# Two VectorE products of Q moved in front of the sums of A's squares, in a kernel whose attention runs under a mixture of experts

## The chip, the core and the metric

The kernel runs on one core of one Trainium2 chip. The metric is the device time of one launch in microseconds. Three runs of the kernel before took 1014.55, 1015.66 and 1016.92 us; their median, 1015.66 us, is the time that the changed kernel is set against.

## The reference, cut to what matters

There are two stages. The first is a linear attention with a complex, per-position decay; the second puts every token through all four experts of a two-layer network and weights the results.

```
mag   = sqrt(a_re^2 + a_im^2);  scale = min(mag, 0.999) / (mag + 1e-6)
ar, ai = a_re * scale, a_im * scale
for t in range(768):                     # state S is complex, 48 x 48 per batch and head
    S_re, S_im = ar*S_re - ai*S_im + k[t] v[t]^T,  ar*S_im + ai*S_re
    y[t] = q[t] . S_re
x   = y as 3072 rows of 384
p   = probs / (sum(probs) + 1e-9)
out = sum over e of p[e] * (relu(x @ w1[e]) @ w2[e])
```

All data are float32; batch 4, heads 8, head size 48, hidden size 1024.

## The kernel before

The 3072 positions are cut into twelve groups of 256 (g = 0 to 11), each of two chunks of 128. In place of the recurrence the kernel works with prefix products of the decay: with A the running complex product of a inside a chunk, the state at a position is A times a sum of k v^T / A, so that attention becomes Q = A q, K = A k / |A|^2 and ordinary matrix products of Q and K.

For each group the work that prepares Q and K runs in this order, mostly on VectorE and ScalarE. `norm` scales a to the allowed magnitude (its ScalarE steps are L320, L321, L331, L332, L337, L339 and L343, its VectorE steps L322, L338, L341, L344, L346). `prefix` forms the running products on VectorE: seven steps (L354 to L357), five doubling steps and a last "fm" step of six products (L305 to L310, 128x651). `finish` then has two parts. `head` lets ScalarE square both parts of A (L416, L417), lets VectorE sum the squares chunk by chunk (L420, below called the reductions), lets ScalarE form 1/|A|^2 by a logarithm and an exponential (L422, L423), and lets VectorE multiply A by q, one product for the real and one for the imaginary part (L425, the Q products). `tail` lets VectorE refine the reciprocal and multiply it by k (L439 to L441) and form the two parts of K (L443).

Q and K then change their layout by way of HBM: SyncE issues Q to `q_d` (L453) and `q_d` back to `Qst` (L460), and likewise `k_d` and `Kst`. `attention` has TensorE transpose K (L494), form state increments (L512), scores from `Qst` and `Kst` (L524) and outputs (L538, L543). Its result y goes to HBM (L611) and comes back as `xa` (L159), and ScalarE and VectorE split it into two parts, `xha` and `xla` (L166, L168). Groups 2 to 5 (`HALF`) send Q and K chunk by chunk, groups 6 to 11 whole.

The expert layers run beside this. For each group TensorE makes eight steps over the hidden size of the first two experts: `w1_step` (L179, into `ph`), then ScalarE's relu (L188, `hh`), VectorE's remainder (L189, `hl`), and `w2_step` (L198, into `po`), which is queued one step later. The attention of group g runs inside the expert steps of group g - 1. A generator hands out the pieces of `norm`, `prefix`, `head` and `tail` at a rate set by constants (`STEP`, `MORE`, `FIRST` and the number that each `yield` carries). The other two experts run at the end for all groups (L836 to L860).

The order of instructions on each engine is not the order in the source alone. A planner takes the traced program, simulates it with its own costs, and issues, engine by engine, what is ready, earlier source first. `behind(ins, prev)` adds an edge of order alone: `ins` stands later than `prev` in its engine's queue and waits for nothing. Each engine works its queue in order, and SyncE issues its transfers in order too. The scratch tiles of `norm`, `prefix` and `finish`, and the tile Q, share four buffers of one tag; a new tile waits until an old one of them is free, and Q's is free when its trip to `q_d` has landed.

Of the kernel before, what the change touches and what calls it, by code (L numbers as in the profile page):

```python
# [11 lines left out]
ALU = mybir.AluOpType  # L12
# [9 lines left out]
C = 128  # L22
# [35 lines left out]
NSEL = 2  # L58
# [10 lines left out]
def fast_path(ctx, tc, qkP, aP, vP, probsP, w, out, flag):  # L69
    nc = tc.nc  # L70
# [38 lines left out]
    def behind(ins, prev):  # L109
        tc.add_manual_dep(ins.ins, prev.ins.name,  # L110
                          mybir.DependencyInfo(mybir.DependencyClass.NoSync, mybir.DependencyReason.DATA),
                          reason="issue order")
# [116 lines left out]
    with ExitStack() as c1:  # L229
# [4 lines left out]
        def tmp(name):  # L234
            return big.tile([P, 2, NJ * G], F32, tag="tmp", name=name, bufs=TMP)
# [30 lines left out]
        def load_a(g, parts=((0, SEG),), prev=None):  # L266
            A = big.tile([P, 2, SEG, MS], F32, tag="A", name=f"A{g}", bufs=NA)
            src = aP[g].rearrange("p (c i m) -> p c i m", c=2, i=SEG)
            for lo, hi in parts:
                for c in range(2):  # L270
                    ins = nc.sync.dma_start(A[:, c, lo:hi], src[:, c, lo:hi])
                    if prev is not None:
                        behind(ins, prev)
            return A

        def load_qk(g, prev=None):
            t = big.tile([P, 2, SEG, MS], F32, tag="qk", name=f"qk{g}", bufs=1)
            src = qkP[g].rearrange("p (c i m) -> p c i m", c=2, i=SEG)
            for c in range(2):
                ins = nc.sync.dma_start(t[:, c], src[:, c])  # L280
                if prev is not None:
                    behind(ins, prev)
            return t
# [106 lines left out]
        def finish(g, A, qk):  # L390
            s = tmp(f"s2{g}")
            u = tmp(f"u2{g}")
            Q = big.tile([P, 2, NR, C + 1], F32, tag="tmp", name=f"Q{g}", bufs=TMP)
            K = []

            def im(ap):
                return ap.rearrange("p (i m) -> p i m", i=SEG)

            def some(ap, lo, hi):
                if hi - lo == CG:  # L400
                    return ap.rearrange("p i m -> p (i m)")
                return ap.rearrange("p i (j c s) -> p i j c s", j=NJ, c=CG)[:, :, :, lo, :]

            def rows(ap, lo, hi):
                if hi - lo == CG:
                    return ap.rearrange("p i (n s) -> p i n s", s=CS)
                return some(ap, lo, hi)

            def dst(ap, lo, hi):
                x = ap.rearrange("p n (i s) -> p i n s", i=SEG)  # L410
                return x if hi - lo == CG else x[:, :, lo::CG, :]

            a2a, i0a, b2a, ta = im(s[:, 0]), im(u[:, 0]), im(s[:, 1]), im(u[:, 1])

            def head(lo, hi):
                nc.scalar.activation(some(a2a, lo, hi), some(A[:, 0], lo, hi), AF.Square)  # L416
                nc.scalar.activation(some(b2a, lo, hi), some(A[:, 1], lo, hi), AF.Square)  # L417
                for c in range(lo, hi):
                    a2, ic = some(a2a, c, c + 1), some(i0a, c, c + 1)
                    red = nc.vector.tensor_tensor_reduce(a2, a2, some(b2a, c, c + 1), scale=1.0, scalar=3e38,  # L420
                                                         op0=ALU.add, op1=ALU.min, accum_out=st_a2[:, c, g:g + 1])
                    nc.scalar.activation(ic, a2, AF.Ln, scale=2.0 ** A2_LOG[c], bias=a2b)  # L422
                    last_act = nc.scalar.activation(ic, ic, AF.Exp, scale=-1.0, bias=a2e[:, c:c + 1])  # L423
                for c in range(2):
                    ins = nc.vector.tensor_tensor(dst(Q[:, c, :, :C], lo, hi), rows(A[:, c], lo, hi),  # L425
                                                  rows(qk[:, 0], lo, hi), op=ALU.mult)
                    if g < NSEL and lo == 1:
                        behind(ins, red)
                if hi == CG:
                    nc.scalar.activation(Q[:, :, :, C].rearrange("p c (j n) -> p c j n", n=CG),  # L430
                                         A[:, :, SEG - 1, NS - 1::NS].unsqueeze(3).broadcast_to([P, 2, NJ, CG]),
                                         AF.Copy)
                return last_act

            def tail(lo, hi):
                if not K:
                    K.append(big.tile([P, 2, NR, C], F32, tag="K", name=f"K{g}", bufs=1))
                a2, i0, t, kn = (some(x, lo, hi) for x in (a2a, i0a, ta, qk[:, 1]))
                nc.vector.tensor_tensor(t, a2, i0, op=ALU.mult)  # L439
                nc.vector.scalar_tensor_tensor(t, t, 2.0, i0, op0=ALU.subtract, op1=ALU.mult)  # L440
                nc.vector.tensor_tensor(t, kn, t, op=ALU.mult)  # L441
                for c in range(2):
                    last_dve = nc.vector.tensor_tensor(dst(K[0][:, c], lo, hi), rows(A[:, c], lo, hi), rows(ta, lo, hi),  # L443
                                                       op=ALU.mult)
                return last_dve

            return Q, K, head, tail

        def trip(nm, X, dst, lo=0, hi=CG, prev=None):
# [210 lines left out]
        A = [load_a(0, halves)]  # L660
        wst = {i: stage1(i, PRE) for i in range(NST)}
        qk = load_qk(0)
# [150 lines left out]
    with ExitStack() as c2:  # L813
# [51 lines left out]
        for r in range(NT // T2):  # L865
            xh, xl = load_x2(r)
            prev = [fin.tile([P, C2, HD], F32, name=f"prev{e}") for e in range(E1)]
# [209 lines left out]
```

## Time and profile before

| What | Value |
|---|---|
| median of three runs | 1015.66 us (1014.55 to 1016.92) |
| the profiled execution's own time | 1011.7 us |
| its span | 1009.9 us |
| TensorE (PE) busy | 979.9 us, 97% |
| weight loads (PEld) | 921.2 us, 91% |
| VectorE (DVE) busy | 590.5 us, 58% |
| ScalarE (ACT) busy | 364.2 us, 36% |
| granted clock of TensorE, whole span | 0.994 |

The span is the time from the first to the last instruction of the program; the own time is what the run's clock gave for the same execution. Busy time says how long an engine had an instruction in it. The last 450 us of the span hold the two experts at the end, where VectorE and ScalarE have little to do, so that their shares over the whole span tell little of the stretch from 110 to 560 us, in which groups 2 to 11 are prepared.

### The profile page before, as it was taken

How to read it: one execution, taken by the hardware profiler on the slowest of the kernel's cores; microseconds unless marked ns; L12 is line 12 of the kernel's file. 1: busy time of each engine (PE TensorE's matmuls, PEld its weight loads, DVE VectorE, ACT ScalarE, POOL GpSimd, SP SyncE). 2: the span in 40 equal slices, each digit the busy share in tenths (PEclk: the TensorE clock that was granted, in tenths of full speed). 3: DMA queues.
4: the chain of work that ended last, by engine and by line, in shares of the span. 5: the costliest groups of instructions: out<-in, count | busy, mean ns of one | idle time of the engine just before them, and what ended most of it. 6: DMA issues, size and time to landing. Idle time of an engine off the chain costs nothing.

```text
span 1009.9 us, 16264 instructions
## 1 busy us (share of the span) xinstructions
PE 979.9 (97%) x6624; PEld 921.2 (91%) x6624; DVE 590.5 (58%) x1229; ACT 364.2 (36%) x653; POOL 34.2 (3%) x64
## 2 busy tenths in 40 slices
PE   4799999999999999999999999999999999999997
PEld 2699999999999999999999999999999899989996
DVE  7798988899988978798942463232132322321221
ACT  7756426446264462636422352121111211211110
POOL 5020000000000000000000000000000000000000
PEclk9899999999999999999999999999999999999999
DMA  9474366573774846547161780020030110100001
GB/s 317 151 148 147 80 160 159 152 187 108 166 184 131 211 96 172 153 123 211 55 168 39 249 307 32 1 94 32 1 126 1 39 56 1 63 1 1 32 1 35
DMA packets 88532, 110.76 MB, mean 110 GB/s; under 512 B 5824, under 2 KB 72944, under 8 KB 88448
## 3 DMA queue, kind: packets, MB, share of 16 engines
q1 hardware_dynamic: 84160, 94.50, 33.4%
q0 software_dynamic: 4288, 15.13, 5.0%
q8 instruction: 54, 0.88, 0.4%
q14 instruction: 30, 0.25, 0.1%
HBM read 73.70 MB, written 35.90 MB: 109 GB/s over the span
## 4 chain that ended last, share of the span: by engine, by line
PE 92%; DVE 2%; ACT 2%; DMA 2%; POOL 1%; issue 0%; DVEq 0%; POOLq 0%; SPq 0%
PE pob L849 20%; PE phb L836 20%; PE ph L179 20%; PE po L198 19%; PE sc L524 4%; PE dp L512 3%; PE yp L543 2%; PE yp L538 2%; PE ktp L494 1%; PE xp L574 1%; DMA mask_d<-mask 1%; DMA maskp<-mask_d 0%; PE qp L385 0%; POOL maskp L246 0%; DMA xa<-y_d 0%
## 5 line engine op out<-in xcount | busy, mean ns | idle before, releaser
L842 DVE SCALAR_TENSOR_TENSOR hlb<-phb,hhb 128x512 fp32r<-128x512 f32 x96 | 66.3, 691 | 270.6 <-ACT hhb L841 270.6
L841 ACT ACTIVATE hhb<-phb 128x512 fp32r<-128x512 f32 x96 | 57.4, 598 | 314.4 <-PE phb L836 299.1
L849 PE MATMUL pob<-wlo,hhb 128*128 128x384 f32 x384 | 129.2, 337 | 0.0
L198 PE MATMUL po<-whi,hh 128*128 128x384 f32 x384 | 129.2, 338 | 0.0
L849 PE MATMUL pob<-whi,hhb 128*128 128x384 f32 x384 | 128.9, 336 | 0.0
L198 PE MATMUL po<-wlo,hh 128*128 128x384 f32 x384 | 128.7, 335 | 0.0
L198 PE MATMUL po<-whi,hl 128*128 128x384 f32 x384 | 124.1, 338 | 0.7 <-DVE hl L189 0.6
L849 PE MATMUL pob<-whi,hlb 128*128 128x384 f32 x384 | 120.4, 336 | 0.0
L188 ACT ACTIVATE hh<-ph 128x512 fp32r<-128x512 f32 x96 | 57.2, 596 | 155.2 <-PE ph L179 145.9
L179 PE MATMUL ph<-xha,whi 128*128 128x256 f32 x576 | 104.5, 287 | 0.8 <-ACT xha L166 0.8
L179 PE MATMUL ph<-xha,wlo 128*128 128x256 f32 x576 | 101.5, 283 | 0.0
L179 PE MATMUL ph<-xla,whi 128*128 128x256 f32 x576 | 101.1, 284 | 0.0
L189 DVE SCALAR_TENSOR_TENSOR hl<-ph,hh 128x512 fp32r<-128x512 f32 x96 | 66.0, 687 | 55.8 <-ACT hh L188 55.4
L836 PE MATMUL phb<-xhb,whi 128*128 128x512 f32 x288 | 91.8, 392 | 0.0
L179 PEld LDWEIGHTS ph<-xha,whi 128*128 128x128 f32 x576 | 86.0, 190 | 2.0 <-ACT xha L166 1.0
L179 PEld LDWEIGHTS ph<-xha,wlo 128*128 128x128 f32 x576 | 83.0, 190 | 0.2 <-issue 0.2
L836 PE MATMUL phb<-xlb,whi 128*128 128x512 f32 x288 | 82.8, 392 | 0.0
L179 PEld LDWEIGHTS ph<-xla,whi 128*128 128x128 f32 x576 | 82.6, 191 | 0.0
L836 PE MATMUL phb<-xhb,wlo 128*128 128x512 f32 x288 | 82.3, 393 | 0.0
L849 PEld LDWEIGHTS pob<-whi,hhb 128*128 128x128 f32 x384 | 72.1, 188 | 3.6
L849 PEld LDWEIGHTS pob<-wlo,hhb 128*128 128x128 f32 x384 | 72.1, 188 | 3.3
L198 PEld LDWEIGHTS po<-whi,hh 128*128 128x128 f32 x384 | 72.4, 189 | 0.4 <-issue 0.3
(165 smaller groups left out, 1569.8 us busy)
## 6 DMA issues: line engine op xcount, KB each, us to landing
wst<-w SPq DMA_DIRECT2D x25, 384.0 KB, 6.1
qk<-qkP SPq DMA_DIRECT2D x24, 384.0 KB, 7.2
acc_d<-acc POOLq DMA_DIRECT2D x24, 384.0 KB, 4.4
prev<-acc_d SPq DMA_DIRECT2D x24, 384.0 KB, 4.7
A<-aP SPq DMA_DIRECT2D x22, 384.0 KB, 8.2
q_d<-Q SPq DMA_DIRECT2D x12, 387.0 KB, 4.1
Qst<-q_d SPq DMA_DIRECT2D x12, 387.0 KB, 6.1
v<-vP SPq DMA_DIRECT2D x24, 192.0 KB, 2.4
```

Of the source, the lines that this page charges most:

```text
L179: ins = nc.tensor.matmul(ph[:, u, :], wt[:, j * P:(j + 1) * P], xt[:, j, :], start=(n == 0), stop=(n == 3 * NJ - 1))
L188: wts["hh"] = nc.scalar.activation(hh, ph, AF.Relu)
L189: nc.vector.scalar_tensor_tensor(hl, ph, 0.0, hh, op0=ALU.max, op1=ALU.subtract)
L198: nc.tensor.matmul(po[t], ht[:, u, t * P:(t + 1) * P], wt[:, HD:], start=(i % FE == 0 and n == 0), stop=(i % FE == FE - 1 and n == 2))
L512: nc.tensor.matmul(d_ps[:, h, :], KT[:, h, :], vc[:, h * D:(h + 1) * D], start=True, stop=True)
L524: nc.tensor.matmul(s_ps[:, h, :], Kc[:, hf * 4 + h, :], Qc[:, hf * 4 + h, :], start=True, stop=True)
L538: ins = nc.tensor.matmul(yo, st[:, o:o + n], Qc[:, o // D, :], start=True, stop=False)
L543: ins = nc.tensor.matmul(yo, vc[:, o:o + n], sc[h // 4][:, h % 4, :], start=first, stop=True)
L836: nc.tensor.matmul(ph, wt[:, j * P:(j + 1) * P], xt[:, j, :], start=(n == 0), stop=(n == 3 * NJ - 1))
L841: nc.scalar.activation(hh, ph, AF.Relu)
L842: nc.vector.scalar_tensor_tensor(hl, ph, 0.0, hh, op0=ALU.max, op1=ALU.subtract)
L849: ins = nc.tensor.matmul(po[t], ht[:, t * P:(t + 1) * P], wt[:, HD:], start=(i % FE == 0 and n == 0), stop=(i % FE == FE - 1 and n == 2))
```

## The change

From group 2 on (`NSEL` is 2) the two Q products are traced directly behind the two squares and in front of the reductions, and an edge of order puts each reduction behind the second product. Groups 0 and 1 keep the old order. No instruction is added or taken away, no size and no buffer changes.

```diff
+                def products(prev=None):
+                    for c in range(2):
+                        ins = nc.vector.tensor_tensor(dst(Q[:, c, :, :C], lo, hi), rows(A[:, c], lo, hi),
+                                                      rows(qk[:, 0], lo, hi), op=ALU.mult)
+                        if prev is not None:
+                            behind(ins, prev)
+                    return ins
+
+                if g >= NSEL:
+                    q = products()
                 for c in range(lo, hi):
                     a2, ic = some(a2a, c, c + 1), some(i0a, c, c + 1)
                     red = nc.vector.tensor_tensor_reduce(a2, a2, some(b2a, c, c + 1), scale=1.0, scalar=3e38,
                                                          op0=ALU.add, op1=ALU.min, accum_out=st_a2[:, c, g:g + 1])
+                    if g >= NSEL:
+                        behind(red, q)
                     nc.scalar.activation(ic, a2, AF.Ln, scale=2.0 ** A2_LOG[c], bias=a2b)
                     last_act = nc.scalar.activation(ic, ic, AF.Exp, scale=-1.0, bias=a2e[:, c:c + 1])
-                for c in range(2):
-                    ins = nc.vector.tensor_tensor(dst(Q[:, c, :, :C], lo, hi), rows(A[:, c], lo, hi),
-                                                  rows(qk[:, 0], lo, hi), op=ALU.mult)
-                    if g < NSEL and lo == 1:
-                        behind(ins, red)
+                if g < NSEL:
+                    products(red if lo == 1 else None)
```

## Rows read from the trace of the kernel before

**Rows 1.** Busy time by stretch: length, engines (instructions), granted clock, DMA share, GB/s.
```profile
110.00:560.00 450.00, 446.98 (x3627) 434.76 (x3626) 362.61 (x792) 208.43 (x383) 10.27 (x19) 1.00 0.55 142
```
**Rows 2.** Waits of TensorE, 110 us to the end: total us, times, longest us.
```profile
PE sc L524 <- issue: 1.5, 2, 0.9
PE ph L179 <- ACT xha L166: 0.8, 1, 0.8
PE po L198 <- DVE hl L189: 0.6, 1, 0.6
```
**Rows 3.** VectorE by line and shape, 110:560: busy us, mean ns | idle before, releaser.
```profile
L425 DVE TENSOR_TENSOR Q<-A,qk 128x768 f32<-128x768 f32 x20 | 18.2, 952 | 0.0
L420 DVE CUSTOM_DVE_ANT_1 s<-s 128x384 f32<-128x384 f32 x20 | 10.4, 555 | 7.5 <-ACT s L417 7.4
L338 DVE TENSOR_TENSOR u<-s,u 128x768 f32<-128x768 f32 x9 | 8.6, 954 | 2.0 <-ACT u L337 1.9
```
**Rows 4.** Waits of ScalarE, 110:560.
```profile
ACT u L332 <- DMA q_d<-Q: 8.9, 6, 2.3
```
**Rows 5.** Timeline of VectorE, group 6: start us, us, instruction [idle before <-releaser].
```profile
279.44 0.83 DVE L310 TENSOR_TENSOR A<-fm_1a,fm_1b 128x651 f32<-128x651 f32 x1
282.79 0.56 DVE L420 CUSTOM_DVE_ANT_1 s<-s 128x384 f32<-128x384 f32 x1 [2.52 <-ACT s L417]
...
284.36 1.82 DVE L425 TENSOR_TENSOR Q<-A,qk 128x768 f32<-128x768 f32 x2
...
292.73 0.69 DVE L189 SCALAR_TENSOR_TENSOR hl<-ph,hh 128x512 fp32r<-128x512 f32 x1 [1.28 <-ACT hh L188]
...
294.34 1.82 DVE L443 TENSOR_TENSOR K<-A,u 128x768 f32<-128x768 f32 x2
```
**Rows 6.** Timeline of ScalarE, group 6.
```profile
288.42 0.92 ACT L331 ACTIVATE s<-s,m2b 128x768 f32<-128x768 f32 x1
...
291.27 0.94 ACT L332 ACTIVATE u<-s,lnb 128x768 f32<-128x768 f32 x1 [1.93 <-DMA q_d<-Q]
292.12 0.58 ACT L188 ACTIVATE hh<-ph 128x512 fp32r<-128x512 f32 x1
```
**Rows 7.** Timeline of SyncE, group 6: issues of transfers.
```profile
295.32 1.24 SPq L453 DMA_DIRECT2D k_d<-K  x2
298.35 1.31 SPq L460 DMA_DIRECT2D Kst<-k_d  x2
```
**Rows 8.** Timeline of TensorE, the first scores of group 6.
```profile
306.46 2.02 PE L524 MATMUL sc<-Qst,Kst 112*128 112x128 f32 x16 [0.86 <-issue]
```
**Rows 9.** Timeline of VectorE, group 2.
```profile
116.53 0.55 DVE L420 CUSTOM_DVE_ANT_1 s<-s 128x384 f32<-128x384 f32 x1
...
126.04 0.96 DVE L338 TENSOR_TENSOR u<-s,u 128x768 f32<-128x768 f32 x1 [0.73 <-ACT u L337]
```
**Rows 10.** Timeline of ScalarE, group 2.
```profile
124.19 0.94 ACT L332 ACTIVATE u<-s,lnb 128x768 f32<-128x768 f32 x1 [1.58 <-DMA q_d<-Q]
```
**Rows 11.** Timeline of TensorE, the first scores of group 2.
```profile
135.29 1.91 PE L524 MATMUL sc<-Qst,Kst 112*128 112x128 f32 x15 [0.64 <-issue]
```
**Rows 12.** Timeline of VectorE, group 4.
```profile
195.93 0.56 DVE L420 CUSTOM_DVE_ANT_1 s<-s 128x384 f32<-128x384 f32 x1 [0.67 <-ACT s L417]
```
**Rows 13.** Timeline of ScalarE, group 4.
```profile
198.54 0.85 ACT L166 ACTIVATE xha<-xa 128x768 fp32r<-128x768 f32 x1 [2.63 <-DMA xa<-y_d]
199.29 0.60 ACT L422 ACTIVATE u<-s,a2b 128x384 f32<-128x384 f32 x1
```
**Rows 14.** Timeline of SyncE, group 4.
```profile
213.82 1.07 SPq L460 DMA_DIRECT2D Kst<-k_d  x2
```
**Rows 15.** DMA issues of 213.5:215, group 4: KB each, median us to landing.
```profile
Kst<-k_d SPq DMA_DIRECT2D x2, 192.0 KB, 3.8
```
**Rows 16.** Timeline of TensorE, the first scores of group 4.
```profile
218.94 2.02 PE L524 MATMUL sc<-Qst,Kst 112*128 112x128 f32 x16
```
**Rows 17.** The nine loads of `xa` by source line L159, from issue to landing.
```profile
DMA to landing us min/median/max: 3.2/3.4/6.6
```

## The prediction

> **What bounds the kernel now.** I read the table of stretches first. Between 110 and 560 us, where groups 2 to 11 are prepared, TensorE has an instruction in it for 446.98 of 450 us, while VectorE is busy for 362.61, which is 81%, and ScalarE for 208.43 [rows 1]. The reader should see that TensorE sets the pace there, and that VectorE is busy but has 87 us to spare. After 560 us the change has no instruction.
>
> The waits of TensorE come second, because only they can be shortened by a new order on VectorE. From 110 us to the end there are four: two in front of scores, 1.5 us together, one of 0.8 us for `xha`, and one of 0.6 us for `hl` [rows 2], in all 2.9 us of a span of 1009.9. That is the ceiling of what the profile lets this change win.
>
> Third I looked at the waits that the change touches directly. VectorE stands idle for 7.4 us in front of the reductions, because they need ScalarE's squares; the twenty Q products, 952 ns each, stand behind them and wait for nothing [rows 3]. One step further on, ScalarE stands idle for 8.9 us, six times, in front of the exponential of the next `norm`, until a trip of Q to `q_d` has landed and Q's buffer is free [rows 4]. Everything behind that exponential on ScalarE, the relu of the experts among it, is held up as well.
>
> **The change part by part.** Nothing is added. Twenty products of 952 ns [rows 3] change places with twenty reductions, two against two in each of ten groups.
>
> *VectorE's own time.* A pair of Q products takes 1.82 us, two reductions about 1.1 us (2 x 555 ns). In group 6 VectorE ends the prefix at 280.27 and waits until 282.79 for the squares [rows 5]. The pair fits into these 2.52 us, the reductions start when they did before, and Q is ready at 282.09 instead of 286.18. Over the ten groups the idle time that can be filled is at most 7.4 us. On TensorE that is worth nothing by itself, since VectorE has 87 us to spare.
>
> *Where a chain reaches TensorE: group 6.* The scores of group 6 start at 306.46 after 0.86 us of idle time [rows 8]. The view has no releaser for it; I take `Kst`, the last of their inputs to be issued, at 298.35 and in the 1.31 us after [rows 7]. Backwards from there: `Kst` follows `k_d`, issued at 295.32 when the first K product has ended; that product stands at 294.34, behind an `hl` at 292.73 for which VectorE was idle for 1.28 us; that `hl` needs the relu at 292.12, which stands on ScalarE behind the exponential at 291.27, which waited 1.93 us for the trip of Q [rows 5 to 7]. This trip ended 5.1 us after the Q products (291.27 less 286.18). With Q 4.1 us earlier it ends at about 287.2, before the logarithm in front of the exponential does (288.42 + 0.92 = 289.34) [rows 6]. The exponential then waits for nothing, the relu comes up to 1.93 us earlier, the `hl` 1.28 us earlier, K likewise. The 0.86 us on TensorE go, and the next thing that is late is TensorE's own queue. Bounds: 0 (the relu's matmuls are not done by then, or something else gates K) to -0.86; I take -0.86.
>
> *Group 2.* The scores wait 0.64 us at 135.29 [rows 11]. VectorE waits 0.73 us in front of K's last products for a `norm` step on ScalarE [rows 9], and that one comes after an exponential that waited 1.58 us for Q's trip [rows 10]. Here, though, VectorE does not idle in front of the reduction at 116.53 [rows 9], so Q moves up by only 1.1 us (the two reductions), while the reductions move back by up to 1.82 us, and with them the logarithms and exponentials for which K's `tail` waits. The first effect takes up to 0.73 us off K's chain, the second adds up to 1.1 us (1.82 less the 0.73 that VectorE got back). Bounds: -0.64 to +1.1 on TensorE; I take -0.3, since the reduction's delay lies partly beside other work that ScalarE has in hand.
>
> *Group 4 (and 5).* VectorE's idle time in front of the reduction is 0.67 us [rows 12], so the reductions move back by 1.82 - 0.67 = 1.15 us, to about 197.1. The logarithm stands on ScalarE behind `xha`, which waits 2.63 us for the load of `xa` and ends at 199.39 [rows 13], so that this delay is covered. The cover matters, because `Kst` here is just in time: its second issue ends at 214.89, lands about 3.8 us later, at some 218.4 to 218.7, and the scores start without a wait at 218.94 [rows 14 to 16]. Without it up to 1.15 - 0.4 = 0.75 us would fall on TensorE. With Q's products begun at 195.26 instead of some 197.0 (195.93 and two reductions) Q's trip runs beside the load of `xa`, which took 3.2 to 6.6 us with a median of 3.4 [rows 17]; I take +0.1 for that.
>
> *The rest.* The 0.8 us for `xha` and the 0.6 us for `hl` [rows 2] belong to ScalarE's order behind the squares and to `xa`; I see nothing in the change that moves them, and count 0 (bounds -1.4 and +0.5, the length of one reduction that may now stand in front of an `xla`). SyncE's queue keeps its members; only Q's issues move up, past `xa` in some groups.
>
> *Sum.* -0.86 - 0.3 + 0.1 = -1.1 us. The profiled execution took 1011.7 us by its own clock and 1009.9 us in span; 1011.7 - 1.1 = 1010.6. It lies 4.0 us below the median of 1015.66, and I carry the difference over unchanged: 1015.66 - 1.1 = 1014.6 us.
>
> **Two rules against the rows.** TensorE's four waits leave 2.9 us to win [rows 2]. The Trainium skill, page "Perfetto Trace Analysis", section "Identifying the Most-Contended Engine", holds that matmul busy time is no good measure of headroom and that the busy time of weight loads is. By that measure the same stretch shows 450 - 434.76 = 15.24 us [rows 1], and an estimate by it would allow a gain down to about 1000. The waits with a named cause bear out the smaller figure; no row here ties the rest to VectorE.
>
> The loads of `xa` took 3.4 us in the middle and 6.6 at most [rows 17]. The Trainium skill, page "DMA: Bandwidth & Descriptors", section "Issuing engines are not separate DMA queues", says that all transfers end up on the same 16 DMA engines and interleave. If that governs here, an earlier Q trip lengthens `xa`; that is the slower rival below.
>
> **The rivals.**
>
> *Nothing reaches TensorE.* The planner pins only the reductions; `hl`, mask products or state updates may stand between prefix and Q, and K may be gated by its own exponentials. For it: `Kst` as the releaser in group 6 is my inference. Against it: the three waits line up in group 6 within 2 us. Time: 1015.7.
>
> *More than the sum.* Both score waits go, and with ScalarE's 8.9 us [rows 4] the `xha` and `hl` waits shrink too: -2.9, so 1012.8. For it: `hl` is VectorE's, which gets up to 7.4 us back [rows 3]. Against it: the larger of the two waits is put down to `xha` [rows 2], which stands on ScalarE beside the squares, and those do not move.
>
> *Slower: the earlier Q trip delays `xa`.* Place: groups 4 and 5, where ScalarE has `xha` in its queue in front of the logarithms [rows 13] and `Kst` lands about 0.4 us before the scores [rows 14 to 16]. Price: `xa` can take up to 6.6 - 3.4 = 3.2 us longer [rows 17]; everything on ScalarE behind `xha` shifts with it, K too, and TensorE waits for what exceeds the 0.4 us, up to 2.8 us in group 4 and as much in group 5. It decides once `xa` is over 0.4 us late. With one of the two groups hit in full and little gained elsewhere: 1015.66 + 2.8 = 1018.4. For it: the ends of rows 17 lie far apart. Against it: a trip that starts when a load of 3.4 us is already under way can hardly double it.
>
> **How the numbers follow.** About 0.2%, or 2.0 us, is what a measurement of this kernel can tell from no change: faster means below 1013.6, slower above 1017.7. The forecast gets 0.52, of which 0.05 lies below 1013.6 and the rest within; nothing reaching TensorE 0.15, all of it within; more than the sum 0.15, of which 0.14 is faster; slower 0.18, of which 0.16 is outside. That makes 0.19 faster, 0.65 the same, 0.16 slower. The forecast alone spans 1013.5 to 1015.8 (-2.2 to +0.1). The range reaches into both outer rivals: 1012.5 to 1017.9, the lower end at the ceiling of 2.9 us, the upper at a loss of some 2.2 us.
>
> **What would show it.** In the changed kernel's timeline VectorE should go from the prefix's last product straight to two Q products in groups 2 to 11, and the 7.4 us in front of the reductions should fall below 2. ScalarE's 8.9 us for Q's trip should fall below 4. In group 6 the `hl` in front of K should have no idle time, K should end about 1.3 us earlier and the scores should start without a wait. In group 2 the score wait should shrink to about 0.3 us. TensorE's waits from 110 us on should add up to about 1.8 us. The prediction is wrong if the score waits stay with K earlier (then `Kst` was not the releaser), if new waits of TensorE of 1 us and more stand in groups 4 and 5, or if TensorE's order itself has changed, which I take it has not.

## The result and the profile after

The changed kernel took 1016.81 us in the median of 22 runs, the kernel before 1013.93 us in as many. One run of the changed kernel, at 1085.55 us and a granted clock of 0.85, was in a slow state and stays out of the comparison. The ratio is 1.0026, with a 95% interval of 1.0015 to 1.0038: it is slower, by about 2.6 us, where -1.1 us was forecast. The profiled execution took 1017.57 us by its own clock and 1015.9 us in span, 6.0 us above the profiled execution before. That is more than twice the typical difference, since the execution profiled before lies 2.2 us below its kernel's median; what follows divides the 6.0 us of this pair of traces.

On VectorE the change did what it says. The first fence holds its rows by line and shape, as in [rows 3]: the idle time in front of the reductions fell from 7.4 us to 0.7 us. The second, ScalarE's waits, answers to [rows 4]: the exponential waits for Q's trip once, 2.7 us in all, where it waited six times and 8.9 us. The third is [rows 1] again: VectorE and ScalarE are as busy as before, and TensorE has an instruction in it for 444.87 us of 450, 2.11 us less than before.

```profile
L421 DVE TENSOR_TENSOR Q<-A,qk 128x768 f32<-128x768 f32 x20 | 18.3, 950 | 0.0
L431 DVE CUSTOM_DVE_ANT_1 s<-s 128x384 f32<-128x384 f32 x20 | 10.3, 553 | 0.7 <-ACT s L417 0.7
```
```profile
ACT xha L166 <- DMA xa<-y_d: 8.1, 2, 5.0
ACT u L332 <- DMA q_d<-Q: 2.7, 1, 2.7
```
```profile
110.00:560.00 450.00, 444.87 (x3590) 430.76 (x3589) 362.46 (x791) 206.94 (x380) 10.08 (x19) 1.00 0.55 141
```

TensorE's waits, the view of [rows 2], show where the gain went. The score waits fell from 1.5 us to 0.5 us, as the prediction wanted, but the waits for `xha` grew from 0.8 us to 2.8 us and those for `hl` from 0.6 us to 1.2 us: 5.0 us in all, where there were 2.9 us.

```profile
PE ph L179 <- ACT xha L166: 2.8, 2, 1.8
PE po L198 <- DVE hl L189: 1.2, 3, 0.7
PE sc L534 <- issue: 0.5, 2, 0.3
PE po L198 <- ACT hh L188: 0.3, 1, 0.3
PE ktp L504 <- DVE K L453: 0.2, 1, 0.2
```

Two places carry most of it. If the first `ph` products of the same expert step are set side by side in the two timelines, the changed kernel is 0.05 us late where the kernel before stands at 143.6 us, 2.6 us late at 164.3 us, 5.0 us late at 320.3 us, and 6.0 us late at the end. (Times after group 2 are therefore to be compared with 2.6 us taken off.)

*The first place is group 2's x, near 158 us.* In the timeline of TensorE seventeen products of the experts (`po`) stand between group 2's first outputs `yp` and the rest, where twelve stood, and only four behind them, where twelve stood. The rest of the outputs begins at 153.07 us in place of 151.62 us, ScalarE's copy y of them starts at 154.88 us in place of 153.43 us, and with it `xha` moves back. TensorE waits 1.80 us for it in place of 0.80 us. The first two rows below are of the kernel before, those of the second fence of the changed kernel. Behind that wait the granted clock is 0.51 for 3.5 us (the third fence, a stretch of the table by stretch), the level of 1.2 GHz, and the same products start 213 ns apart where they did 120 ns. That costs another 1.5 us.

```profile
151.62 0.43 PE L543 MATMUL yp<-scs,v 128*64 128x128 f32 x4
...
157.81 0.62 PE L179 MATMUL ph<-xha,whi 128*128 128x256 f32 x3 [0.80 <-ACT xha L166]
```
```profile
136.43 2.02 PE L534 MATMUL sc<-Qst,Kst 112*128 112x128 f32 x16 [0.17 <-issue]
...
153.07 0.43 PE L553 MATMUL yp<-scs,v 128*64 128x128 f32 x4
...
158.94 0.62 PE L179 MATMUL ph<-xha,whi 128*128 128x256 f32 x3 [1.80 <-ACT xha L166]
...
296.52 0.63 PE L179 MATMUL ph<-xha,whi 128*128 128x256 f32 x3 [1.03 <-ACT xha L166]
...
309.82 2.02 PE L534 MATMUL sc<-Qst,Kst 112*128 112x128 f32 x16 [0.34 <-issue]
```
```profile
160.00:163.50 3.50, 3.50 (x19) 3.50 (x18) 1.64 (x4) 2.30 (x4) 0.00 (x0) 0.51 0.87 236
```

*The second is group 6's Q beside group 5's x, near 296 us.* SyncE's timeline follows, first before (three rows), then after. Group 6's Q trip now stands among the two `y_d` stores and in front of the load `xa`, which before went first, at 284.41 us, with Q at 285.37 us. The second store lands 5.0 us after its issue (before 2.5 us), and `xa`, issued when it has landed, takes 6.4 us (before 3.2 us). Over all nine loads of `xa` the median went from 3.4 us [rows 17] to 5.6 us. ScalarE stands idle for 5.00 us in front of `xha`. That makes K late, since its `tail` waits on VectorE behind `xla`: K's first product starts at 299.11 us, where it started at 294.34 us [rows 5], so that K is 2.2 us later still than the 2.6 us that the kernel is late already.

```profile
280.57 1.67 SPq L611 DMA_DIRECT2D y_d<-y  x2
284.41 0.38 SPq L159 DMA_DIRECT2D xa<-y_d  x1
285.37 1.19 SPq L453 DMA_DIRECT2D q_d<-Q  x2
```
```profile
283.26 0.33 SPq L621 DMA_DIRECT2D y_d<-y  x1
283.68 0.40 SPq L463 DMA_DIRECT2D q_d<-Q  x1
284.17 0.73 SPq L621 DMA_DIRECT2D y_d<-y  x1
284.99 1.15 SPq L463 DMA_DIRECT2D q_d<-Q  x1
...
289.19 0.36 SPq L159 DMA_DIRECT2D xa<-y_d  x1
290.80 0.31 SPq L470 DMA_DIRECT2D Qst<-q_d  x1
300.09 1.23 SPq L463 DMA_DIRECT2D k_d<-K  x2
```
```profile
DMA to landing us min/median/max: 3.5/5.6/7.1
```
```profile
282.44 1.82 DVE L421 TENSOR_TENSOR Q<-A,qk 128x768 f32<-128x768 f32 x2
...
296.50 0.96 DVE L168 TENSOR_TENSOR xla<-xa,xha 128x768 fp32r<-128x768 f32 x1 [4.93 <-ACT xha L166]
...
299.11 1.82 DVE L453 TENSOR_TENSOR K<-A,u 128x768 f32<-128x768 f32 x2
```
```profile
295.62 0.84 ACT L166 ACTIVATE xha<-xa 128x768 fp32r<-128x768 f32 x1 [5.00 <-DMA xa<-y_d]
```

### The profile page after: what moved, and what is told of

Same layout as the page of the kernel before. It is cut to its first block, busy times and chain, and to the rows that moved or that the text cites. A ratio compares the mean times of both kernels' runs of the same rounds, so it can differ in the third digit from the quotient of the medians.

```text
span 1015.9 us, 16263 instructions
## 1 busy us (share of the span) xinstructions
PE 984.0 (97%) x6624; PEld 923.0 (91%) x6624; DVE 590.7 (58%) x1229; ACT 363.9 (36%) x653; POOL 34.4 (3%) x64
## 4 chain that ended last, share of the span: by engine, by line
PE 88%; DMA 4%; DVE 3%; ACT 2%; POOL 1%; issue 1%; DVEq 0%; POOLq 0%; SPq 0%
PE pob L859 20%; PE phb L846 20%; PE po L198 18%; PE ph L179 18%; PE sc L534 4%; PE dp L522 2%; PE yp L553 2%; PE yp L548 2%; PE ktp L504 1%; DMA xa<-y_d 1%; DMA y_d<-y 1%; DMA q_d<-Q 1%; PE xp L584 1%; DMA mask_d<-mask 1%; PE qp L385 0%
## 5 line engine op out<-in xcount | busy, mean ns | idle before, releaser
L198 PEld LDWEIGHTS po<-whi,hl 128*128 128x128 f32 x384 | 70.9, 188 | 2.7 <-DVE hl L189 2.5
```

Of the source, the lines that this page charges most:

```text
L198: nc.tensor.matmul(po[t], ht[:, u, t * P:(t + 1) * P], wt[:, HD:], start=(i % FE == 0 and n == 0), stop=(i % FE == FE - 1 and n == 2))
```

## The experiments

Each ratio is against the kernel before, run on the same chip. A profile shows one execution. In six traces (the kernel before and five of the kernels below) not one instruction up to group 2's scores stands in another order, and their wait was still between nothing and 1.65 us. So verdicts rest on the ratios, and the traces say where to look.

**Which groups.** `g >= NSEL` was replaced by a list of groups.

```diff
-                if g >= NSEL:
+                if g in QF:        # (2,)  (2, 3)  (3,)  (6,)  or (3, 4, 5, 7, 8, 9, 10, 11)
                     q = products()
```

> The kernel before with the Q products in front in group 2 alone. TensorE's and ScalarE's orders up to 160 us then are those of the changed kernel but for the place of group 3's reductions. Theory 1 (TensorE's new order, which leaves 4 expert matmuls instead of 12 behind the outputs of group 2, makes the wait for xha long): the wait near 158 us is 1.6 to 1.9 us, as in the changed kernel, and the score wait of group 2 is 0.1 to 0.7 us; 0.5 to 2 us above before, more with a stretch of half clock behind the wait. Theory 2 (group 3's reductions behind its Q products make ScalarE late): the wait stays at 0.8 us and the time is that of before.

> The kernel before with the Q products in front in group 6 alone. Theory 1 (the trip of Q runs beside the store of y and the load of xa and slows both): the second y_d store takes about 5 us instead of 2.5, xa 6 to 7 instead of 3.2, ScalarE waits 4 to 5 us for xa, TensorE waits 1 to 1.7 us for xha near 293 us and loses 1 us more in the matmuls behind; the scores of group 6 wait 0.1 to 0.4 instead of 0.86 us; 1.5 to 2.5 us above before, ratio 1.0015 to 1.0025, and nothing is changed near 158 us. Rival (the slow xa of the changed kernel is the trace's accident, or comes from the other groups' shifted traffic): xa below 5 us, ratio within 0.0005 of 1.

> The kernel before with the Q products in front in group 3 alone; TensorE's order is then exactly that of before. Theory 1: the wait for xha near 158 us stays at 0.8 us, no other wait of TensorE grows by more than 0.2 us, ratio 0.999 to 1.001. Theory 2: 0.5 us or more is added in waits for xha, or for hh with ScalarE's logarithms waiting for the reductions for over 0.5 us; ratio up to 1.001.

> The kernel before with the Q products in front only in groups 2 and 3; the rest as before. Theory 1: the loss near 159 us is there in full (wait of 1.8 us for xha instead of 0.80, half clock for some 3 us, 2.5 us together), the score wait of group 2 is 0.2 instead of 0.64 us, and nothing is lost near 293 us: 1.5 to 2.2 us above before, ratio 1.0015 to 1.002. Rival (a loss spread over all groups): two tenths of the whole, 0.5 us, ratio 1.0005.

Group 2 alone: 1.0021 (1.0010 to 1.0032). Group 6 alone: 1.0027 (1.0016 to 1.0038). Group 3 alone: 1.0007 (0.9990 to 1.0024), no loss that can be told. Groups 2 and 3: 1.0016 (0.9998 to 1.0035). The theories held for groups 2 and 6, for group 6 just past their upper ends (1.8 us, 1.0027). The waits of TensorE, first in the kernel with group 2, then in that with group 6, show each place by itself: one `xha` wait of 1.7 us near 160 us in the first, one of 1.8 us at 294.64 us, behind an `xa` of 7.6 us, in the second.

```profile
PE sc L535 <- issue: 1.7, 2, 1.0
PE ph L180 <- ACT xha L167: 1.7, 1, 1.7
```
```profile
PE ph L180 <- ACT xha L167: 2.6, 2, 1.8
PE sc L535 <- issue: 1.8, 2, 1.2
```

> The change in groups 3 to 5 and 7 to 11 alone; groups 2 and 6 keep the old order. Theory (the loss sits in groups 2 and 6): ratio 0.9990 to 1.0005, TensorE's wait for xha near 158 us stays at about 0.8 us, none near 294 us, no load of xa over 4 us next to group 6, the score wait of group 6 stays at 0.6 to 1.0 us. Rival (every group loses a little): ratio 1.001 or more, with a new wait of TensorE of 1 us or more in one of the other groups, or TensorE's own time longer without a wait.

This theory fell: 1.0022 (1.0006 to 1.0038) without a change in groups 2 and 6. Its trace has the longest wait, 2.88 us, in front of group 6's scores, though groups 2 and 6 are as before. The planner gave TensorE there nearly the order that it gives with group 6 alone: some 2.3 us of expert products stand behind the scores that stood in front of them. The scores are due at 303.3 us in place of 305.6 us, and `Kst` still lands at 306.1 us.

```profile
302.05 1.28 PE L523 MATMUL dp<-v,KT 128*112 128x48 f32 x12
306.21 3.75 PE L535 MATMUL sc<-Qst,Kst 112*128 112x128 f32 x16 [2.88 <-issue]
```

**Half of the change.** One product in front of the reductions and one behind, in all groups from 2 on.

```diff
-                def products(prev=None):
-                    for c in range(2):
+                def products(prev=None, cs=(0, 1)):
+                    for c in cs:
```

> The changed kernel with only the first Q product of each group in front of the reductions and the second behind them. The idle time in front of the reductions is 0.7 us per group in the mean and one product takes 0.95, so the reductions come at most 0.3 us later, and Q 0.95 us earlier. If the loss is lateness of the reductions (theory 2): the time is that of before or 0.5 us better, ratio 0.9995 to 1.0005. If it is what the planner makes of TensorE's and SyncE's orders (theory 1): in group 6 the first half of Q's trip still goes out in front of xa (here even in front of both stores of y), so the loss near 293 us stays, 1 us or more, ratio 1.001 to 1.002.

1.0036 (1.0022 to 1.0050), from 5 runs: no cheaper than the whole, and above both ranges. Theory 2 falls; of theory 1 the `xha` wait near 294 us stayed, 1.0 us, and one of 1.3 us stands near 157 us.

**The two places put back in the changed kernel.** For group 6 the Q trip was put behind the load of group 5's `xa` in SyncE's queue, for group 2 the `po` products behind the last output, each by edges of order, and then both.

```diff
+                if g == 6:
+                    qb = trip(f"q_d{g}", Q, Qst, prev=wts["xa", g - 1])
```
```diff
+                    if pin is not None:      # pin: the last yp of group 2, for group 1's last step
+                        behind(ins, pin)
```

> The changed kernel with one thing put back: in group 6 the two transfers of Q to q_d stand behind the load of group 5's xa in SyncE's queue, as they did before; the orders of TensorE, VectorE and ScalarE stay those of the changed kernel. Theory 1 (the earlier Q trip of group 6 holds the load of xa back, because a Qst transfer that waits for the trip stands in front of it): xa is issued within 0.1 us of the landing of y_d, ScalarE's wait for it falls from 5.0 to under 2 us, TensorE's wait of 1.03 us for xha near 296 us goes, with the 1.0 us of shorter waits behind it, and the time lies 1.5 to 2.7 us below the changed kernel, near 1.000 to 1.001 of before. Rival (the reductions, now behind the Q products, make the logarithms, K and hl late): TensorE's lost time near 296 us stays within 0.5 us of the 2.7 us it has in the changed kernel, ratio still 1.002 to 1.003.

> The changed kernel with one thing put back: eight expert matmuls (po of the last step of group 1) stand behind the outputs yp of group 2 in TensorE's queue, as they did before, and not in front of them. Theory 1 (the planner's new order on TensorE leaves only 4 of these matmuls to cover the way from yp over ScalarE to xha): the wait for xha near 159 us falls from 1.80 to 0.8 us or less, the 3.3 us of half clock behind it (granted clock 0.51) do not occur, TensorE gets 2 to 2.6 us back there, ratio 1.000 to 1.001 of before. Rival (ScalarE's xha is late because the squares and the reductions of group 3 are): the wait stays above 1.4 us, the clock still falls, ratio 1.002 to 1.003.

> The changed kernel with both things put back (SyncE's order in group 6, TensorE's order at group 2's outputs). Theory 1: what is left is VectorE's filled idle time and the shorter waits in front of the scores of groups 2 and 6 (about 1 us together): 0.5 to 1.5 us below before, ratio 0.9985 to 0.9995. Rival (lateness from the reductions in all groups): ratio 1.001 to 1.003.

1.0018 (0.9997 to 1.0040), 1.0009 (0.9993 to 1.0025) and 1.0009 (0.9989 to 1.0029): each lower than the change as made, but no interval clears either kernel, and the gain that the theory had for both together (0.9985 to 0.9995) didn't show. The waits went as the theories said. In the first trace `xa` took 3.8 us and no `xha` wait stood at 294 us; in the second the `xha` wait at group 2's outputs was 0.58 us; in the third both were so, but the scores of group 6 waited 2.0 us. The same holds over all traces: the six kernels with Q's stores in front of `xa` have an `xha` wait of 1.0 to 3.5 us there, and no other has one.

The first trace shows one thing more, because in it the forecast chain came true up to K. ScalarE's exponential starts at 288.64 us without a wait, in place of 291.27 us [rows 6], and K 2.9 us earlier (first product at 291.46 us, before at 294.34 us [rows 5]). (The exponential does not wait for Q's second store at all in this kernel: that landed at 291.16 us.) But K's store now ran beside both `Qst` transfers and took 5.5 us where it took 3.1 us, so that `Kst` was issued at 297.88 us, 0.5 us earlier than before, and the scores still waited 0.95 us. In three more kernels whose K was stored while both `Qst` transfers were under way (groups 3 to 5 and 7 to 11 alone, both things put back, and SyncE's old order below) the store took 5.5 to 6.1 us.

```profile
288.64 0.92 ACT L332 ACTIVATE u<-s,lnb 128x768 f32<-128x768 f32 x1
```
```profile
291.46 1.82 DVE L453 TENSOR_TENSOR K<-A,u 128x768 f32<-128x768 f32 x2
```
```profile
289.49 2.01 SPq L470 DMA_DIRECT2D Qst<-q_d  x2
292.45 1.25 SPq L463 DMA_DIRECT2D k_d<-K  x2
297.88 1.32 SPq L470 DMA_DIRECT2D Kst<-k_d  x2
```

**Group 2 with TensorE's order put back.**

> The change in group 2 alone, with the second expert products of group 1's last step held behind group 2's outputs on TensorE, as they stood in the kernel before. Theory (group 2's loss is TensorE's changed order, its gain the shorter score wait): the xha wait near 158 us falls from the 1.7 us of group 2 alone to 0.5 to 0.9 us, the score wait is about 0.4 us, ratio 0.9990 to 1.0005. Rival (the reductions that now come later cost it on ScalarE, whatever TensorE's order): a wait for hh or hl of about 1 us stands in the place of the xha wait, ratio 1.001 or more.

0.9987 (0.9974 to 1.0000), against 1.0021 without the pin (the edge of order that holds the `po` products back); the `xha` wait is 0.6 us, and the rival's wait for `hh` is 0.5 us. For group 2 the loss was TensorE's new order. Over all traces the `xha` wait there is 1.7 to 1.8 us in the five with that order, 1.3 us with half of the change, and 0.6 to 0.9 us in all others. (The 2.2 us in front of scores stand at group 6, which this kernel doesn't change.)

```profile
PE sc L537 <- issue: 2.2, 1, 2.2
PE ph L180 <- ACT xha L167: 0.6, 1, 0.6
PE po L199 <- ACT hh L189: 0.5, 1, 0.5
```

**All orders held.** To see the swap without the planner, every instruction of an engine was put behind the one that stood before it in the kernel before; on VectorE the two products stand in front of the two reductions. The table of orders makes the line numbers larger.

```diff
+        for e, runs in ORDER.items():      # the order of the kernel before, as (first, count)
+            had = getattr(QU, "q" + e)     # the engine's instructions as they were traced
+            order = [had[a + i] for a, k in runs for i in range(k)]
+            for ins, prev in zip(order[1:], order):
+                behind(ins, prev)
```

> The change in all groups 2 to 11, but with the whole order of instructions of TensorE, ScalarE and SyncE held as in the kernel before, and VectorE's too except that the two Q products stand in front of the two sums: the swap and nothing that the planner does on top of it. Theory (the loss is the planner's new orders and the earlier transfers, not the swap): ratio 0.9985 to 1.0003, the xha wait near 158 us 0.6 to 1.0 us, none near 294 us, both score waits shorter than before (under 0.5 us each). Rival (the later sums cost it themselves, through the logarithms on ScalarE): ratio 1.001 or more, with new waits of TensorE for hh, hl or scores.

The theory fell again, and the rival held: 1.0032 (1.0017 to 1.0047) for the swap by itself. Most of VectorE's idle time in front of the reductions is gone (0.8 us is left of 7.4 us), but ScalarE, whose logarithms need the reductions, now stands idle for 12.7 us waiting for them, where it stood 4.6 us (the first two fences: before, then the held swap).

At group 2 the reductions start at 118.12 us (before 116.53 us [rows 9]) and K's products at 125.89 us where they started at 124.29 us. Counted from the prefix's last product, K starts 1.7 us later in all three kernels with this swap in the old orders, and not at all later in the six traces named above. The scores wait 1.27 us in place of 0.64 us here and 1.48 and 2.96 us in the other two, against nothing to 1.65 us in the six.

At group 6 Q is ready at 282.05 us, four microseconds earlier, but its two stores go out at 285.13 and 285.65 us in place of 285.37 and 286.20 us, because `xa` stands in front of them in SyncE's queue; they land after 6.0 and 6.4 us in place of 5.0 us, and ScalarE's exponential starts 0.9 us later than in [rows 6]. K, `k_d` and `Kst` follow, and the scores wait 2.01 us, with the granted clock at 0.50 from 309 to 312 us. That the swap made these stores slow isn't shown: in the kernel below that doesn't swap group 6 they took 6.5 and 6.8 us, and its scores waited 2.2 us. The other fences: VectorE at group 2, SyncE and ScalarE at group 6, TensorE.

```profile
ACT u L422 <- DVE st_a L420: 4.6, 7, 1.2
```
```profile
ACT u L625 <- DVE st_a L621: 12.7, 8, 2.9
```
```profile
116.38 1.82 DVE L611 TENSOR_TENSOR Q<-A,qk 128x768 f32<-128x768 f32 x2
118.12 0.55 DVE L621 CUSTOM_DVE_ANT_1 s<-s 128x384 f32<-128x384 f32 x1
```
```profile
284.64 0.38 SPq L349 DMA_DIRECT2D xa<-y_d  x1
285.13 0.96 SPq L653 DMA_DIRECT2D q_d<-Q  x2
```
```profile
292.17 0.94 ACT L522 ACTIVATE u<-s,lnb 128x768 f32<-128x768 f32 x1 [2.34 <-DMA q_d<-Q]
```
```profile
135.77 2.02 PE L724 MATMUL sc<-Qst,Kst 112*128 112x128 f32 x16 [1.27 <-issue]
...
307.66 2.69 PE L724 MATMUL sc<-Qst,Kst 112*128 112x128 f32 x16 [2.01 <-issue]
```

> As the kernel with all orders held, but SyncE issues group 6's Q transfers among the stores y_d and in front of the load xa of group 5, as the changed kernel does; nothing else differs. Theory (transfers that run together slow each other): the second y_d store takes 4 us or more, xa 6 us or more, a wait of TensorE for xha of 1 to 1.8 us near 294 us, time 1 to 4 us above that kernel. Rival (the transfers did not matter, the new order on TensorE did): xa under 4.5 us or no wait for xha, time within 0.7 us of that kernel.

The theory held in kind, and the loss was larger than it said: 1.0076 (1.0053 to 1.0099, from 6 runs), 5.3 us above the held swap, by the order of seven transfers alone. The second `y_d` store took 4.0 us, `xa` 6.8 us (3.5 us in the held swap), and TensorE waited 3.53 us for `xha`, with the granted clock at 0.50 for the next 3.5 us.

```profile
300.73 1.01 PE L370 MATMUL ph<-xha,whi 128*128 128x256 f32 x3 [3.53 <-ACT xha L357]
```
```profile
300.70:304.20 3.50, 3.47 (x16) 3.47 (x17) 3.45 (x5) 3.47 (x5) 0.00 (x0) 0.50 0.00 0
```

> The swap with all orders held, in groups 3 to 5 and 7 to 11 only; groups 2 and 6 keep VectorE's old order. Theory (the swap costs at group 2, through the sums that come later, and at group 6, through Q's stores that run beside xa; elsewhere it is neutral): ratio 0.9990 to 1.0008, the xha wait near 158 us at 0.8 us, the score waits of groups 2 and 6 no longer than 0 to 1.0 us. Rival (the other groups lose a little each): ratio 1.0015 or more, with waits of TensorE at other groups.

1.0012 (0.9994 to 1.0030): below the held swap in all groups, but it does not reach the theory's 1.0008 nor the rival's 1.0015, and the scores of group 6, not swapped in it, waited 2.23 us in its trace, behind an `xa` of 6.0 us. ScalarE stood idle for 11.2 us in front of the logarithms in it, so most of that idle time lies where TensorE feels little of it. Whether the other groups cost a little stays open.

**One queue's old order in the changed kernel.**

> The changed kernel with SyncE's order of the kernel before; TensorE's order stays the changed one. Theory: no xha wait near 294 us, the wait of 1.7 us near 158 us stays, ratio 1.0005 to 1.002. Rival (the transfers are the whole loss): ratio 0.9995 or less. Rival (TensorE's order is the whole loss): ratio 1.0025 or more.

> The changed kernel with TensorE's order of the kernel before throughout; the other engines' orders are as the planner then makes them. Theory: the xha wait near 158 us is 0.6 to 1.0 us, an xha wait near 294 us of 1 us or more stays where the Q transfers of group 6 stay early, ratio 1.0005 to 1.002. Rival (TensorE's order is the whole loss): ratio 0.9995 or less. Rival (it is no part of it): ratio 1.0025 or more.

1.0051 (1.0030 to 1.0071) and 1.0045 (1.0022 to 1.0067). Both theories fell, and both ratios lie where one rival each had put them: the one that TensorE's order is the whole loss, and the one that it is no part of it. They can't both be true, so the losses don't add. Nor is either kernel better than the change as made (their intervals overlap). With SyncE's old order there is no `xha` wait at 294 us, but TensorE, which comes to group 6's scores earlier in its new order, waits 2.5 us there; with TensorE's old order the early Q trip still costs an `xha` wait of 1.3 us, and an `hl` wait of 1.3 us follows it.

**Is `Kst` slowed by later loads?** The four loads of qk and A that SyncE issues behind group 6's `Kst` were moved behind the next load of v, in the kernel before, in the held swap, and in group 2 alone with its pin; all other orders were held.

```diff
-    Kst(6), Kst(6), qk(7), qk(7), A(8), A(8), v(7)
+    Kst(6), Kst(6), v(7), qk(7), qk(7), A(8), A(8)
```

> The kernel before with every queue's order held, except that the four loads of the next groups' qk and A, which SyncE issues directly behind group 6's Kst, stand behind the next load of v. Theory (group 6's scores wait for Kst, and Kst for its share of the DMA engines, not for Q or K to be ready): Kst lands in 4.5 us or less in place of 4.7 to 7.0, the score wait of 0.86 us near 306 us goes, ratio 0.9970 to 0.9995. Rival (Kst is set by when K is ready, as the prediction had it): the score wait stays at 0.6 us or more, ratio 0.9995 to 1.0005. Rival (the loads are then late themselves): new waits near 325 us, ratio over 1.001.

> The swap with all orders held, with the same four loads behind v. Theory: the score wait of 2.0 us of the held swap falls below 0.3 us and its time by 2 to 4 us, to a ratio of 0.998 to 1.0005; what then remains above the kernel before with late loads is the price of the swap itself. Rival (the swap's loss is VectorE's or ScalarE's): ratio 1.002 or more, score wait gone or not.

> The change in group 2 alone with the expert products held behind the outputs, and with the four loads of group 6 behind v. Theory: no score wait of 0.3 us or more at group 2 or 6, ratio 0.996 to 0.9985, below both kernels. Rival (run to run spread gave that kernel its 0.9987): ratio as the kernel before with late loads, or above it.

1.0005 (0.9988 to 1.0021), 1.0032 (1.0017 to 1.0047) and 1.0002 (0.9989 to 1.0014). The theory fell: `Kst` took 4.4 to 6.9 us without these loads beside it, as against 4.7 to 7.0 us with them, and the score wait stayed at 0.75 us. In that the prediction was right: `Kst` is as late as K was ready and stored. The held swap lost the same 0.32% again. Group 2 alone with its pin, here on another chip and with late loads, took 1.0002, so its 0.9987 is no gain to rely on. No version here beats the kernel before by more than its interval; group 2 alone with its pin, at 0.9987, comes nearest.

## Why the prediction was wrong, step by step

*VectorE's time and ScalarE's wait for Q.* Right in size: 7.4 us to 0.7 us ("below 2"), 8.9 us to 2.7 us ("below 4"). The second is partly luck. In group 6 the exponential waits for nothing of Q's, but starts at 296.37 us, because it stands behind `xha` and its wait of 5.00 us; with all orders held the wait for Q fell only to 6.3 us. And VectorE's idle time was not won: with the orders held 8.1 us more of it stood on ScalarE (4.6 to 12.7 us). The prediction had said for group 6 that "the reductions start when they did before", and looked at later reductions in groups 2 and 4 (and 5) alone.

*"With Q 4.1 us earlier it ends at about 287.2."* This is the step that failed in group 6. Q was ready four microseconds earlier, and that alone was carried over to its trip, with its stores, `xa` and K's store counted at their old lengths. In the held swap the stores could leave only 0.24 and 0.55 us earlier, because `xa` stood ahead of them, and they landed 0.9 us later. With the queue's order changed as well they left earlier, and `y_d` (2.5 to 5.0 us) and `xa` (3.2 to 6.4 us) paid for it, so that K came later and not 1.28 us earlier. And where K did come earlier, with Q's trip behind `xa`, its store took 5.5 us in place of 3.1 us, and the scores still waited 0.95 us. The DMA engines were busy for 0.70 of the time from 283 to 296 us before and for 0.92 in the changed kernel (the last but one figure of the rows below, stretches of the table by stretch): the stretch had free time, but transfers that run together took longer each.

```profile
283.00:296.00 13.00, 13.00 (x93) 13.00 (x92) 11.53 (x18) 9.88 (x16) 0.00 (x0) 1.00 0.70 163
```
```profile
283.00:296.00 13.00, 12.48 (x89) 12.16 (x87) 6.30 (x12) 7.57 (x13) 0.00 (x0) 1.00 0.92 217
```

*Group 6's scores, -0.86 us.* The releaser was right: the scores begin 0.08 to 0.09 us after the last `Kst` lands in every trace looked at in which they waited. The sign came out by luck. The wait is 0.34 us, but K's first product was later, at 299.11 us in place of 294.34 us; TensorE itself came 3.9 us later (309.82 less 0.34, against 306.46 less 0.86). What the wait lost was more than spent some ten microseconds ahead of it, at `xha`.

*Group 2's scores, -0.3 us.* The wait went from 0.64 us to 0.17 us, but not by the way described. With the orders held, the effect that the prediction priced at "up to 1.1 us" won: K came 1.7 us later, and the scores waited 1.27 to 2.96 us in three traces. In the changed kernel the planner put five `ph` products of the experts in front of the scores, which covers part of the wait, and the price of its new order is the `xha` wait behind group 2's outputs.

*Groups 4 and 5, +0.1 us.* No wait appeared at group 4's scores. The slower rival was a real mechanism, put in the wrong place: it hit group 5's x through group 6's Q, where a whole trip of two 387 KB stores meets the `y_d` stores, and it reached TensorE through `xha` and not through `Kst`. Its argument against, that a trip starting beside a load under way "can hardly double it", was wrong twice: the trip starts before the load, which then waits for a slowed `y_d`, and the load did double, 3.2 us to 6.4 us. That rival had a chance of 0.18, and its 1018.4 us lies nearer to the measured time than the forecast's 1014.6 us. The Trainium skill, page "DMA: Bandwidth & Descriptors", section "Issuing engines are not separate DMA queues", says that transfers run on the same 16 DMA engines and interleave, whichever engine started them; these numbers, all of SyncE's transfers, agree.

*"The rest", counted 0, and TensorE's order, "which I take it has not" changed.* This is the step that failed at group 2, where the pair of traces parts by 2.6 of its 6.0 us. The planner, which simulates the whole program, answered a swap on VectorE with a new order on TensorE; the `xha` waits counted at 0 grew from 0.8 us to 2.8 us, and the `hl` waits from 0.6 us to 1.2 us. Putting its one edit at group 2's outputs back took 1.0021 to 0.9987.

*The ceiling of 2.9 us* bounded the gain, but nothing of the kind bounded the loss: waits of TensorE that were not there before, priced only in the slower rival, and the half clock behind them, which the prediction did not price at all.

What stays open: how the 2.6 us divide in a typical run. The groups measured one at a time (0.21% for group 2, 0.27% for group 6, 0.22% for the others) add up to far more than the whole, 0.26%, and the swap alone, without the planner's orders, costs 0.32%. That each new wait shifts what the next one meets would explain it, but isn't shown.

## What to carry to other kernels

Where a planner orders the queues, an edit on one engine is also an edit on all others: compare the planned orders of each queue before counting a step as untouched, and hold them to learn what the edit itself is worth. When the next step of a chain is a transfer, being ready earlier is worth only what the queue ahead of it and the transfers beside it leave: here Q was ready 4.1 us earlier and its stores left 0.24 and 0.55 us earlier, and a K store moved beside `Qst` took 5.5 us for 3.1 us. Read both before carrying a gain through a transfer. And ask of a swap what moves back, not only what moves up: here two reductions of 0.55 us that moved back 1.6 us held up K by as much.

## What the runs showed of the hardware that was not expected

A wait of TensorE can cost about as much again behind it. After the 1.80 us wait at 158 us the granted clock was 0.51, the lower level, for 3.5 us, some 1.5 us of lost time; after the 3.53 us wait at 300.73 us it was 0.50. It does not always come: the kernel with Q's trip behind `xa` waited 1.80 us at the same place, and the 5 us behind it were granted in full.

A transfer of one size can take twice as long beside others: `xa` (384 KB) took 3.0 us at the least and 7.6 us at the most over the traces here at the same place, and group 6's K store 2.6 us and 6.1 us.

A score wait of 2.2 us at group 6 appeared in two executions whose TensorE order there was the old one (group 2 alone with its pin, and the held swap without groups 2 and 6), where the kernel before waited 0.86 us; the granted clock of the 5 us behind was 0.50 in both. Single profiles can differ by this much with no edit at the place.
